# The first stage of a fused Fourier filter and MLP: first DFT in groups of 4 with two evacuations side by side, W loaded first, tables cleared by GpSimd

## Chip, cores, metric

One core of a Trainium2 chip. The time is the device time of one execution in microseconds (us), median of several executions. An interval is a 95% interval of a ratio of two kernels.

## The reference

For 8 batches of 3008 x 256: a real Fourier transform along the sequence, a complex 256 x 256 matrix with bias, a soft threshold, the inverse transform, then an MLP with a squared ReLU.

```python
def _attn_ref(x, w_r, w_i, b_r, b_i):
    X = np.fft.rfft(x, axis=1)
    Yr = Xr @ w_r - Xi @ w_i + b_r
    Yi = Xr @ w_i + Xi @ w_r + b_i
    lam = 0.01
    Yr = np.sign(Yr) * np.maximum(np.abs(Yr) - lam, 0.0)     # Yi alike
    y = np.fft.irfft(Y, n=x.shape[1], axis=1)

def _moe_ref(x, w_in, w_out, s, b):
    r = np.maximum(x @ w_in, 0.0)
    return (s * (r * r) + b) @ w_out
```

The kernel does the transform of length 3008 as 94 x 32, with tables: `A_t` for the first DFT of each column, `F_c` for the forward DFT over 32, `T_c` for its inverse, `C_t` for the last one.

## The kernel before

Only the first batch matters here. Its stages: x comes in four chunks of 8 columns (n2); each chunk gets 2 x 8 first-DFT matmuls into a PSUM tile of two banks, and four copies ("evacuations") of it into `ut`; when all of `ut` is there, the *mix* multiplies it by W; then the forward DFT needs the mix's result `g` and the table F spread out as `F_t` (by ACT) and `F_2` (by DVE).

```python
    def emit_load_x(b):
        for c in range(N2 // XCH):                     # four chunks of 8 n2
            t = xpool.tile([P, XCH * D], F16, name="x16", tag="x16")
            nc.gpsimd.dma_start(out=t[0:N1, :], in_=xv[:, c * XCH * D : (c + 1) * XCH * D])
    ...
    A_t = ...; emit_load_x(0)                          # W is not loaded here
    ...
    def first_batch():
        keep_awake(36)                                 # matmuls on ones, for the PE clock
        for c in range(N2 // XCH):
            for dc in range(DC):
                ps = two_banks()
                for j in range(XCH):
                    last_pe = nc.tensor.matmul(ps[:, j // 4, ...], x16[(0, c)][...], A_t[0:N1, :], ...)
                for h in range(2):
                    on_dve, on_act = evac(ut[:, dc, :, n2 : n2 + 4], ps[:, h, 0:384]..., 384)
            with tc.issue_after(last_pe.ins):
                keep_awake(14 if c < 3 else 10)
            if c == 0:                                 # gate: W only after the first evacuations
                with tc.issue_after(last_dve.ins):
                    for st in w_st:
                        nc.vector.memset(st[0:1, :, 0:D:P], 0.0)
                emit_load_w()
            if c == 1:                                 # gate of F_c (c == 2: T_c, the same way)
                with tc.issue_after(last_dve.ins):
                    nc.vector.memset(F_c[0:1, 0, 0, 0:1], 0.0)
                emit_load_forward()
            ...
            if c == 2:
                place_w(0)                             # ACT copies W to f16, half by half
        place_w(1); place_f(0); place_f_2(0)
```

A gate is a one-element memset of the tile to be loaded, ordered behind an evacuation: the load has to wait for it. `evac` picks ACT or DVE by a running sum of their loads.

Of the kernel before, what the change touches and what calls it, by code (L numbers as in the profile page):

```python
# [14 lines left out]
P = 128  # L15
N1 = 94
N2 = 32
# [79 lines left out]
def kernel(  # L97
# [13 lines left out]
    nc = tc.nc  # L111
    B, S, D = x.shape
# [42 lines left out]
    def evac(dst, src, cols, scale=None):  # L155
        ta, td = 0.17 + cols / 1200.0, 0.15 + cols / 960.0
        if load["act"] + ta <= load["dve"] + td:
            load["act"] += ta
            if scale is None:
                return None, nc.scalar.copy(out=dst, in_=src)  # L160
            return None, nc.scalar.mul(out=dst, in_=src, mul=scale)
        load["dve"] += td
        if scale is None:
            return nc.vector.tensor_copy(out=dst, in_=src), None
        return nc.vector.tensor_scalar_mul(out=dst, in0=src, scalar1=scale), None

    def two_banks():
        return hpool.tile([P, 2, 512], F32, name="psh", tag="psh")

    def one_bank():  # L170
        return fpool.tile([P, 512], F32, name="psf", tag="psf")

    def other_bank():
        return apool.tile([P, 512], F32, name="psa", tag="psa")


    XCH = 8
    x16 = {}

    def emit_load_x(b):  # L180
        xv = x[b].rearrange("(n1 n2) d -> n1 (n2 d)", n2=N2)
        for c in range(N2 // XCH):
            t = xpool.tile([P, XCH * D], F16, name="x16", tag="x16")
            nc.gpsimd.dma_start(  # L184
                out=t[0:N1, :], in_=xv[:, c * XCH * D : (c + 1) * XCH * D]
            )
            x16[(b, c)] = t

    ones = cpool.tile([P, P], F16, name="ones")
    nc.vector.memset(ones, 1.0)  # L190

    def keep_awake(n):

        ps = other_bank()
        for _ in range(n):
            nc.tensor.matmul(ps[:, 0:P], ones, ones, start=True, stop=True)


    A_t = cpool.tile([P, 96], F16, name="A_t")
    nc.sync.dma_start(out=A_t[0:N1, :], in_=A_d)  # L200
    emit_load_x(0)
    W_t = cpool.tile([P, DC, 2, D], F16, name="W_t")
    w_st = []
    for w in (w_r, w_i):
        st = rpool.tile([P, DC, D], F32, name="w_st", tag="rt")
        w_st.append(st)

    def emit_load_w():

        for e in (slice(0, P), slice(P, D)):  # L210
            for w, st in zip((w_r, w_i), w_st):
                nc.sync.dma_start(
                    out=st[:, :, e], in_=w.rearrange("(c p) e -> p c e", p=P)[:, :, e]
                )


    b_g = cpool.tile([P, 2, D], F32, name="b_g")
    nc.vector.memset(b_g, 0.0)
# [21 lines left out]
    def emit_load_forward():  # L240
        nc.sync.dma_start(out=F_c.rearrange("p q r k -> p q (r k)"), in_=F_d)
        nc.sync.dma_start(out=sel_t, in_=S_d)

    def emit_load_inverse():
        t_load = nc.sync.dma_start(out=T_c, in_=T_d)
        with tc.issue_after(t_load.ins):
            nc.sync.dma_start(out=eye_t, in_=E_d)
            nc.sync.dma_start(out=C_t, in_=C_d)
            for i, bv in enumerate((b_r, b_i)):
                nc.sync.dma_start(out=b_st[:, i], in_=bv.unsqueeze(0).to_broadcast([P, D]))  # L250
            nc.sync.dma_start(out=s_bc, in_=moe_s.unsqueeze(0).to_broadcast([P, 1]))
            nc.sync.dma_start(out=bb_bc, in_=moe_b.unsqueeze(0).to_broadcast([P, 1]))
# [18 lines left out]
    nc.vector.memset(T_t, 0.0)  # L271
    F_2 = [uspool.tile([P, H, P], F16, name="F_2", tag="us") for _ in range(2)]
    for f in F_2:
        nc.vector.memset(f, 0.0)

    def make_bounds():
        for t, c in ((low, -LAM), (high, LAM)):
# [11 lines left out]
    def blocks(t):  # L289
        return t.rearrange("p q (r a k) -> p q r a k", r=2, a=2)  # L290

    def place_w(ec):
        e = slice(ec * P, ec * P + P)
        for i in range(2):
            nc.scalar.copy(out=W_t[:, :, i, e], in_=w_st[i][:, :, e])

    def place_f(h):
        q = slice(h * H, h * H + H)
        for a in range(2):
            r = slice(64 * a, 64 * a + 64)  # L300
            nc.scalar.copy(out=blocks(F_t)[r, q, :, a], in_=F_c[r, q])

    def place_f_2(h):

        q = slice(h * H, h * H + H)
        for a in range(2):
            r = slice(64 * a, 64 * a + 64)
            nc.vector.tensor_scalar_mul(
                out=blocks(F_2[h])[r, :, 0, a], in0=F_c[r, q, 1], scalar1=-1.0
            )  # L310
            nc.vector.tensor_copy(out=blocks(F_2[h])[r, :, 1, a], in_=F_c[r, q, 0])
# [27 lines left out]
    def first_batch():  # L339
        ut = ypool.tile([P, DC, 96, N2], F16, name="ut", tag="yt")  # L340
        last_dve = last_act = None
        keep_awake(36)
        for c in range(N2 // XCH):
            for dc in range(DC):
                ps = two_banks()
                for j in range(XCH):
                    lo = j * D + dc * P
                    last_pe = nc.tensor.matmul(
                        ps[:, j // 4, (j % 4) * 96 : (j % 4) * 96 + 96],
                        x16[(0, c)][0:N1, lo : lo + P], A_t[0:N1, :],  # L350
                        start=True, stop=True,
                    )
                for h in range(2):
                    n2 = c * XCH + 4 * h
                    on_dve, on_act = evac(
                        ut[:, dc, :, n2 : n2 + 4],
                        ps[:, h, 0:384].rearrange("p (n k) -> p k n", k=96), 384,
                    )
                    last_dve = on_dve or last_dve
                    last_act = on_act or last_act  # L360
            with tc.issue_after(last_pe.ins):
                keep_awake(14 if c < 3 else 10)
            if c == 0:
                with tc.issue_after(last_dve.ins):
                    for st in w_st:
                        nc.vector.memset(st[0:1, :, 0:D:P], 0.0)
                emit_load_w()
            if c == 1:
                with tc.issue_after(last_dve.ins):
                    nc.vector.memset(F_c[0:1, 0, 0, 0:1], 0.0)  # L370
                emit_load_forward()
            if c == 2:
                with tc.issue_after(last_dve.ins):
                    nc.vector.memset(T_c[0:1, 0, 0:1], 0.0)
                emit_load_inverse()
            if c == 2:
                with tc.issue_after(last_act.ins):
                    place_w(0)
        with tc.issue_after(last_dve.ins), tc.issue_after(last_act.ins):
            place_w(1)  # L380
            place_f(0)
            place_f_2(0)

        gate = nc.gpsimd.tensor_copy(out=w_in_t[0][0:1, 0:1], in_=T_c[0:1, 0, 0:1])
        with tc.issue_after(gate.ins):
            emit_load_x(1)
            emit_load_weights()
# [113 lines left out]
        for i in range(2 * U + 2):  # L501
# [6 lines left out]
            k = i - U - 2  # L508
# [334 lines left out]
    def schedule(start, span, units):  # L843
        for i, u in enumerate(units):
            plan.setdefault(start + (i * span) // len(units), []).append(u)

    more = first_batch()
    load.update(act=0.0, dve=0.0)
    mark = {}
# [3 lines left out]
    schedule(0, 10, more)  # L853
    plan.setdefault(15, []).append(make_bias)
    plan.setdefault(17, []).append(lambda: emit_load_x(2))
    schedule(22, 44, s23_units(1))
    schedule(mark[1] - 14, 12, s4_units(1))
    for b in range(2, B):
        s0, s1, s2 = mark[b - 2], mark[b - 1], mark[b]
        p = s1 - s0  # L860
        schedule(s0 + 40, p - 48, s1_units(b))
        p = s2 - s1
# [47 lines left out]
```

## Time and profile before

| | before |
|---|---|
| time, median of 3 | 853.37 us (853.29 to 853.9) |
| span of the profiled execution | 852.0 us |
| PE busy | 836.7 us (98%) |
| last evacuation of `ut` ends | 16.03 us |
| first forward-DFT matmul | 18.34 us |

From 52 us on PE is full, so what the change can give is the moment at which the first batch gets through its stages. I use two marks for that: the end of the last `ut` evacuation (the first mix matmul that needs it starts 0.05 us later) and the first forward-DFT matmul. Times are from the start of the span.

### The profile page before, as it was taken

How to read it: one execution, taken by the hardware profiler on the slowest of the kernel's cores; microseconds unless marked ns; L12 is line 12 of the kernel's file. 1: busy time of each engine (PE TensorE's matmuls, PEld its weight loads, DVE VectorE, ACT ScalarE, POOL GpSimd, SP SyncE). 2: the span in 40 equal slices, each digit the busy share in tenths (PEclk: the TensorE clock that was granted, in tenths of full speed). 3: DMA queues.
4: the chain of work that ended last, by engine and by line, in shares of the span. 5: the costliest groups of instructions: out<-in, count | busy, mean ns of one | idle time of the engine just before them, and what ended most of it. 6: DMA issues, size and time to landing. Idle time of an engine off the chain costs nothing.

```text
span 852.0 us, 17108 instructions
## 1 busy us (share of the span) xinstructions
PE 836.7 (98%) x6668; PEld 602.7 (71%) x6668; DVE 698.1 (82%) x1027; ACT 643.8 (76%) x860; POOL 32.5 (4%) x54
## 2 busy tenths in 40 slices
PE   8899999999999999999999999999999999999997
PEld 7757777777777766777667776777667777766765
DVE  6888987888878987888878888888977888776674
ACT  5887887787778887787777887787877778666663
POOL 3210000000000000000000000000000000000000
PEclk9999999999999999999999999999999999999999
DMA  7963457424671357424663247613354223411111
GB/s 168 157 155 97 115 138 174 122 77 97 169 195 54 93 151 190 110 78 104 164 159 89 74 106 180 191 39 92 100 155 119 62 78 96 112 32 38 38 44 50
DMA packets 105410, 95.07 MB, mean 112 GB/s; under 512 B 9454, under 2 KB 97778, under 8 KB 103986
## 3 DMA queue, kind: packets, MB, share of 16 engines
q1 hardware_dynamic: 99330, 79.57, 32.3%
q0 software_dynamic: 6000, 14.42, 10.7%
q8 instruction: 52, 0.85, 0.4%
q14 instruction: 28, 0.23, 0.1%
HBM read 52.54 MB, written 46.66 MB: 116 GB/s over the span
## 4 chain that ended last, share of the span: by engine, by line
PE 90%; DVE 4%; ACT 3%; DMA 1%; issue 1%; DVEq 0%; ACTq 0%; POOLq 0%
PE psa L820 37%; PE psh L751 37%; PE psf L617 4%; PE psf L552 3%; PE psf L588 2%; PE psf L603 2%; PE psf L700 2%; PE psf L647 2%; DVE gt L765 1%; ACT rt L758 1%; PE psh L401 1%; DMA w_st<-in_w_r_dram 1%; DMA x<-in_x_dram 1%; ACT yt L160 0%; ACT vs L160 0%
## 5 line engine op out<-in xcount | busy, mean ns | idle before, releaser
L758 ACT ACTIVATE rt<-psh 128x1024 f32<-128x1024 f32 (+2 forms) x384 | 387.1, 1009 | 115.6 <-PE psh L751 114.2
L765 DVE TENSOR_TENSOR gt<-rt 128x1024 f16<-128x1024 f32 (+2 forms) x323 | 386.6, 1200 | 99.4 <-ACT rt L758 98.7
L820 PE MATMUL psa<-w_out_t,gt 128*128 128x256 f16 (+1 forms) x3024 | 453.9, 272 | 0.1
L820 PEld LDWEIGHTS <-gt 128*128 128x128 f16 (+1 forms) x3024 | 301.0, 101 | 186.8 <-issue 1.6
L751 PE MATMUL psh<-yt,w_in 128*128 128x512 f16 (+1 forms) x1344 | 396.9, 378 | 0.0
L751 PEld LDWEIGHTS <-w_in 128*128 128x128 f16 x1536 | 142.8, 98 | 26.6 <-issue 1.7
L830 DVE SCALAR_TENSOR_TENSOR ost<-psa,s_bc,bias_bc 128x512 f32<-128x512 f32 (+1 forms) x96 | 70.9, 738 | 9.6 <-PE psa L820 8.2
L762 ACT ACTIVATE gt<-rt 128x1024 f16<-128x1024 f32 (+2 forms) x61 | 64.1, 1051 | 1.0
L622 DVE TENSOR_TENSOR ring<-psf,s 128x512 f16<-128x512 f32 x84 | 57.5, 685 | 3.5 <-PE psf L617 3.4
L160 ACT CAST v<-psf 128x512 f16<-128x512 f32 x80 | 46.5, 582 | 18.1 <-PE psf L647 18.1
L160 ACT CAST xf<-psf 128x512 f16<-128x512 f32 x82 | 48.0, 585 | 11.1 <-PE psf L588 11.1
L160 ACT CAST u<-psf 96x512 f16<-96x512 f32 x78 | 45.1, 580 | 12.3 <-PE psf L552 12.1
L751 PE MATMUL psh<-tail,w_in 128*128 128x512 f16 (+1 forms) x192 | 52.1, 353 | 0.0
L617 PE MATMUL psf<-W_g,xf 128*128 128x256 f16 x336 | 50.4, 273 | 0.0
L160 ACT CAST yt<-psf 128x480 f16<-128x480 f32 (+2 forms) x76 | 38.5, 518 | 14.4 <-PE psf L700 14.3
L552 PE MATMUL psf<-x,A_t 94*96 94x512 f16 x104 | 39.6, 381 | 1.6 <-ACT yt L160 0.5
L628 DVE TENSOR_TENSOR ring<-ring,high 128x512 f16<-128x512 f16 x84 | 35.5, 423 | 2.2
L629 DVE TENSOR_TENSOR ring<-ring 128x512 f16<-128x512 f16 x84 | 35.5, 422 | 1.9
L627 DVE TENSOR_TENSOR ring<-ring,low 128x512 f16<-128x512 f16 x84 | 35.4, 421 | 1.5
L617 PEld LDWEIGHTS <-xf 128*128 128x128 f16 x336 | 32.9, 98 | 3.7
L184 POOL DMA_DIRECT2D x<-in_x_dram x32 | 16.9, 530 | 461.2 <-PE psf L552 445.1
L700 PE MATMUL psf<-C_t,vs 96*128 96x96 f16 x448 | 32.9, 205 | 0.0
(84 smaller groups left out, 490.7 us busy)
## 6 DMA issues: line engine op xcount, KB each, us to landing
out_dram<-ost SPq DMA_DIRECT2D x152, 128.0 KB
x<-in_x_dram POOLq DMA_DIRECT2D x32, 376.0 KB, 6.0
ud<-u SPq DMA_DIRECT2D x28, 384.0 KB
us<-ud SPq DMA_DIRECT2D x28, 384.0 KB
vd<-v SPq DMA_DIRECT2D x42, 256.0 KB
vs<-vd SPq DMA_DIRECT2D x14, 768.0 KB
ring<-ring SPq DMA_DIRECT2D x280, 32.0 KB
out_dram<-ost SPq DMA_DIRECT2D x16, 120.0 KB
```

The lines of the kernel that those rows point to most:

```text
L160: return None, nc.scalar.copy(out=dst, in_=src)
L552: nc.tensor.matmul(ps[0:96, :], A_t[0:N1, :], x16[(b, c)][0:N1, j * D : (j + 2) * D], start=True, stop=True,)
L617: nc.tensor.matmul(ps[:, r, :], xt[:, 2 - r, dc], W_g[:, dc, r], start=(dc == 0), stop=(dc == DC - 1),)
L622: nc.vector.tensor_tensor(out=t, in0=ps, in1=hold[i // 2][:, i % 2].unsqueeze(1).to_broadcast([P, 2, D]), op=ALU.add,)
L628: nc.vector.tensor_tensor(out=m, in0=m, in1=high, op=ALU.min)
L700: nc.tensor.matmul(ps[:, j * 96 : (j + 1) * 96], vs[(b, h)][:, k, ec * P : (ec + 1) * P], C_t, start=True, stop=True,)
L751: nc.tensor.matmul(o, w_in_t[dc][:, mc * P : (mc + 1) * P], r, start=(dc == 0), stop=(dc == DC - 1),)
L758: nc.scalar.activation(out=rt[:, :, 0:w], in_=ps[:, :, 0:w], func=AF.Relu)
L762: nc.scalar.activation(out=gt[:, :, 0:w], in_=rt[:, :, 0:w], func=AF.Square)
L765: nc.vector.tensor_tensor(out=gt[:, :, 0:w], in0=rt[:, :, 0:w], in1=rt[:, :, 0:w], op=ALU.mult)
L820: nc.tensor.matmul(ps[0:size, h, :], gts[(ti, mc // 2)][:, mc % 2, sub * size : (sub + 1) * size], w_out_t[:, mc, :], start=(mc == 0), sto ...
L830: nc.vector.scalar_tensor_tensor(out=ost[0:size, 0:k], in0=ps[0:size, 0:k], scalar=s_bc[0:size], in1=bias_bc[0:size, 0:k], op0=ALU.mult, o ...
```

## The change

Its intent: let ACT and DVE evacuate at the same time (a tile each), have W there before ACT needs it, start PE after half a chunk, and take clears off DVE.

```diff
@@ x in halves (batch 0 only)
+            parts = 2 if b == 0 else 1
+            for i in range(parts):
+                nc.gpsimd.dma_start(out=t[0:N1, i * w : (i + 1) * w], in_=xv[...])
@@ W at the head of the loads
         st = rpool.tile([P, DC, D], F32, name="w_st", tag="rt")
+        nc.sync.dma_start(out=st, in_=w.rearrange("(c p) e -> p c e", p=P))
-    def emit_load_w(): ...
@@ clears
     for f in F_2:
-        nc.vector.memset(f, 0.0)
+        nc.gpsimd.memset(f, 0.0)
@@ first_batch
-        keep_awake(36)
-        for c in range(N2 // XCH):
+        last_pe = keep_awake(40)
+        for g in range(N2 // 4):
+            c, h = divmod(g, 2)
             for dc in range(DC):
-                ps = two_banks()
+                ps = one_bank() if dc else two_banks()[:, 0]
...                                            (4 matmuls and one evacuation for each dc)
-                keep_awake(14 if c < 3 else 10)
+                last_pe = keep_awake(5)
+            if h == 0:
+                continue
             if c == 0:
-                ... gate of W, emit_load_w()
-            if c == 1:
                 ... gate of F_c, emit_load_forward()   # one chunk earlier
...
-            if c == 2:  place_w(0)                     # and place_w(1) at the end
+            if c == 1:  place_w()                      # whole
```

With W's gate gone, the gate of F_c moves from the second chunk to the first.

More of the change, by code (lines that the diff above doesn't have):

```diff
@@ L183, in emit_load_x @@
             t = xpool.tile([P, XCH * D], F16, name="x16", tag="x16")
-            nc.gpsimd.dma_start(
-                out=t[0:N1, :], in_=xv[:, c * XCH * D : (c + 1) * XCH * D]
-            )
+            parts = 2 if b == 0 else 1
+            w = XCH * D // parts
+            for i in range(parts):
+                nc.gpsimd.dma_start(
+                    out=t[0:N1, i * w : (i + 1) * w],
+                    in_=xv[:, c * XCH * D + i * w : c * XCH * D + (i + 1) * w],
+                )
             x16[(b, c)] = t
@@ L195, in keep_awake @@
         for _ in range(n):
-            nc.tensor.matmul(ps[:, 0:P], ones, ones, start=True, stop=True)
+            mm = nc.tensor.matmul(ps[:, 0:P], ones, ones, start=True, stop=True)
+        return mm
     A_t = cpool.tile([P, 96], F16, name="A_t")
@@ L205 @@
         st = rpool.tile([P, DC, D], F32, name="w_st", tag="rt")
+        nc.sync.dma_start(out=st, in_=w.rearrange("(c p) e -> p c e", p=P))
         w_st.append(st)
-    def emit_load_w():
-        for e in (slice(0, P), slice(P, D)):
-            for w, st in zip((w_r, w_i), w_st):
-                nc.sync.dma_start(
-                    out=st[:, :, e], in_=w.rearrange("(c p) e -> p c e", p=P)[:, :, e]
-                )
     b_g = cpool.tile([P, 2, D], F32, name="b_g")
@@ L290, in blocks, with place_w @@
         return t.rearrange("p q (r a k) -> p q r a k", r=2, a=2)
-    def place_w(ec):
-        e = slice(ec * P, ec * P + P)
+    def place_w():
         for i in range(2):
-            nc.scalar.copy(out=W_t[:, :, i, e], in_=w_st[i][:, :, e])
+            nc.scalar.copy(out=W_t[:, :, i], in_=w_st[i])
     def place_f(h):
@@ L341, in first_batch @@
         last_dve = last_act = None
-        keep_awake(36)
-        for c in range(N2 // XCH):
+        last_pe = keep_awake(40)
+        for g in range(N2 // 4):
+            c, h = divmod(g, 2)
             for dc in range(DC):
-                ps = two_banks()
-                for j in range(XCH):
-                    lo = j * D + dc * P
-                    last_pe = nc.tensor.matmul(
-                        ps[:, j // 4, (j % 4) * 96 : (j % 4) * 96 + 96],
-                        x16[(0, c)][0:N1, lo : lo + P], A_t[0:N1, :],
-                        start=True, stop=True,
-                    )
-                for h in range(2):
-                    n2 = c * XCH + 4 * h
-                    on_dve, on_act = evac(
-                        ut[:, dc, :, n2 : n2 + 4],
-                        ps[:, h, 0:384].rearrange("p (n k) -> p k n", k=96), 384,
-                    )
-                    last_dve = on_dve or last_dve
-                    last_act = on_act or last_act
+                ps = one_bank() if dc else two_banks()[:, 0]
+                with tc.issue_after(last_pe.ins):
+                    for j in range(4):
+                        lo = (4 * h + j) * D + dc * P
+                        mm = nc.tensor.matmul(
+                            ps[:, j * 96 : j * 96 + 96],
+                            x16[(0, c)][0:N1, lo : lo + P], A_t[0:N1, :],
+                            start=True, stop=True,
+                        )
+                last_pe = mm
+                on_dve, on_act = evac(
+                    ut[:, dc, :, 4 * g : 4 * g + 4],
+                    ps[:, 0:384].rearrange("p (n k) -> p k n", k=96), 384,
+                )
+                last_dve = on_dve or last_dve
+                last_act = on_act or last_act
             with tc.issue_after(last_pe.ins):
-                keep_awake(14 if c < 3 else 10)
+                last_pe = keep_awake(5)
+            if h == 0:
+                continue
             if c == 0:
-                with tc.issue_after(last_dve.ins):
-                    for st in w_st:
-                        nc.vector.memset(st[0:1, :, 0:D:P], 0.0)
-                emit_load_w()
-            if c == 1:
                 with tc.issue_after(last_dve.ins):
@@ L375, in first_batch @@
                 emit_load_inverse()
-            if c == 2:
+            if c == 1:
                 with tc.issue_after(last_act.ins):
-                    place_w(0)
+                    place_w()
         with tc.issue_after(last_dve.ins), tc.issue_after(last_act.ins):
-            place_w(1)
             place_f(0)
```

## The prediction

> **What bounds the kernel now.** I read the page first, then busy times in stretches, then the chain of waits over the first 20 us, then the order of DVE and ACT work there, then the DMA view and its packets. The stretches say where time can be won at all:
>
> ```profile
> 0.00:16.00 16.00, 12.30 (x153) 11.46 (x153) 9.21 (x21) 6.36 (x14) 3.38 (x10) 1.00 0.82 180
> 16.00:52.00 36.00, 31.14 (x381) 25.29 (x382) 31.96 (x54) 30.33 (x47) 11.21 (x16) 1.00 0.76 136
> 52.00:200.00 148.00, 147.89 (x1147) 106.34 (x1144) 127.65 (x197) 118.17 (x164) 3.08 (x6) 1.00 0.48 126
> 200.00:837.00 637.00, 635.76 (x4914) 451.94 (x4913) 523.87 (x753) 486.89 (x636) 14.81 (x22) 1.00 0.40 107
> ```
>
> The columns are stretch, length, then busy us of PE, weight loads, DVE, ACT and GpSimd, the clock, the DMA share and GB/s. From 52 us to 837 us PE is busy 783.65 of 785 us: a full pipeline that keeps its length and only moves with its start. From 16 to 52 us the first batch runs through its later stages with DVE and ACT nearly full (32 and 30 of 36 us). The change edits only what comes before that, the first DFT of batch 0. So the question is one number: when does the mix (L401, the first matmul that needs the whole of `ut`) start? Now it is 16.08 us. The chain up to there:
>
> ```profile
> 1.21 4.85 DMA x<-in_x_dram
> ...
> 6.11 1.48 PE psh L348 x16
> ...
> 8.12 0.56 DVE ut L164
> 8.67 0.05 DVE w_st L366 x2
> 8.73 4.99 DMA w_st<-in_w_r_dram
> ...
> 13.79 0.35 ACT W_t L295
> ...
> 14.60 0.39 ACT ut L160
> 14.98 0.02 issue
> 15.00 1.03 DVE ut L164 x2
> 16.04 0.05 issue
> 16.08 1.82 PE psh L401 x15
> ```
>
> Start, length, what. W is loaded only after a DVE memset at 8.67 us that itself waits for the first evacuations. It lands at 13.72, and ACT, which has the copy of W in its queue ahead of its last two evacuations, stands still for it (1.33 us). Then comes a serial tail: ACT copy, ACT evacuation, and two DVE evacuations that wait for ACT's. The list of waits up to 30 us shows that last link four times over:
>
> ```profile
> DVE ut L164 <- ACT ut L160: 5.1, 4, 2.0
> ACT W_t L295 <- DMA w_st<-in_w_r_dram: 1.3, 1, 1.3
> ```
>
> Columns: total us, times, longest. PE is not what runs late: the last eight-by-two block of first-DFT matmuls ran at 12.57 to 13.60, 2.5 us before the mix.
>
> **What the Trainium skill says.** "PSUM — Partial Sum Buffer", section "Specifications (TRN2)": ScalarE and VectorE may read PSUM at the same time at full rate if they are not in one bank. The two evacuations of a tile lie in two banks here, and DVE still waited for ACT in all four chunks; so what orders them is the shared tile, not the memory, and tiles of their own can remove it. "DMA: Bandwidth & Descriptors", section "Issuing engines are not separate DMA queues": all queues run on the same 16 engines; section "Queues, rings and completion order": an engine takes turns between queues packet by packet. The trace agrees with the first half (DMA share 1.05 while x comes in, 5 to 10 us); how x and W would share, no run shows yet. "TensorE: Matmul & The Clock Gate", section "What's actually happening": PE runs at half rate until about 3.4 us of sustained work. The trace agrees: 14 keep-awake matmuls take 1.69 us from 7.37 but 0.95 us from 10.12. "VectorE: DVE Perf Modes", section "Zero memsets can be issued as uint32": half the elements for a 2-byte type. DVE's two F clears are 128x768 uint32 in 1.51 us; on GpSimd they become 128x1536 f16.
>
> **The change, part by part.**
>
> *Evacuations side by side.* Before, a chunk of 8 n2 has two tiles, each with an ACT evacuation (0.48 to 0.53 us) and then a DVE one (0.51 to 0.60). After, a group of 4 n2 has one tile for ACT and one for DVE; the built order shows ACT always on the first, DVE on the second, and neither waiting for the other. A group costs about 0.55 us of evacuation instead of about 1.05 in series. The tail after the last matmul falls from 13.60 -> 16.03 to about one DVE evacuation.
>
> *W at the head.* The memset gate and the 4.99 us landing leave the path; ACT copies W after its fourth evacuation (2 copies of 128x512; 128x256 takes 0.41 us, so about 1.2 us together), between evacuations that ACT has time for. Removed from the path: the 1.33 us wait and, at the end, the 0.8 us of copies ahead of the last evacuations. But nothing is free on the DMA engines. x of batch 0 is 4 x 376 KB = 1.54 MB, and from 3 to 10.5 us its queue moved 1.46 MB at 99.6% of all engines, that is 0.195 MB/us: 7.9 us of pure transfer, the last packets at about 10.8 us in the packet records. In these records a 1024-byte plain packet takes 49 ns and a 3072-byte one 121 ns. W becomes 2 x 256 packets of 1024 bytes: 512 x 49 / 16 = 1.6 us of all engines. It is issued at about 1.1 us, so its packets should start near 2.2 us, and x is dense from about 2.9; I count 0.5 us of it as free and 1.1 us as taken from x.
>
> *F_c earlier.* The gate of the forward table moves from the second chunk (issue 11.44, after x) to the first, about 8 us, inside the x stream: 128 x 121 / 16 = 1.0 us more taken from x. T_c stays at the third chunk, whose packets should start about when x ends.
>
> *x in halves.* Eight loads at 0.53 us of GpSimd issue each = 4.3 us, less than the transfer, so issue is not the bound; the bytes are the same. It lets PE start after half a chunk (about 5.2 instead of 6.1) and, more to the point, leaves only 8 matmuls after the last landing instead of 16.
>
> *Clears by GpSimd.* 1.51 us leave DVE at 5.0 to 6.5, where DVE waited until 7.48 anyway: worth nothing on the path. On GpSimd, from the rows there (128x512 in 0.61 to 1.50 us) I estimate 2 to 4.5 us each, after the bias loads, so the first is done near 11 us; the half F table is needed at about 14.
>
> *Sum.* x ends at 10.8 + 1.1 + 1.0 = 12.9 us; the semaphore at about 13.1 (the first chunk shows some 0.25 us). Then 8 matmuls at 65 ns (16 take 1.03 us) and a start gap, 0.65 us; then one DVE evacuation, 0.55 us: mix at 14.3 us. Against 16.08 that is 1.8 us. Everything behind moves along: the built order of all five engines is identical, line for line, from the mix to the end. Time: 853.4 - 1.8 = 851.6, and I say 851.5.
>
> **Rivals.**
> 1. *The landing of x takes the place of the landing of W.* I hold this to be the new bound in any case; the question is how much it gives back. If W and F_c take their full 2.6 us from x and the half-size packets lose a little more, x ends at 13.5 to 14, the mix starts near 15.3 and the time is 852.6. For it: the DMA share is already 1.0. Against: W is issued before x.
> 2. *x is hardly delayed*, since W fits into the slow ramp of the x queue at 2.5 to 3.5 us and F_c packets queue behind x: x ends near 11.5, mix at 12.9, time 850.2. For it: the engines were half empty (share 0.54) in the first 5 us. Against: packet by packet turns favour the small queue's progress, at x's cost.
> 3. *W lands late instead*, because each of its packets waits for a bigger x packet: then ACT stands at the copy again, now ahead of four evacuations. If W lands by 10.5, ACT needs 1.2 + 4 x 0.48 = 3.1 us: 13.6, no harm; by 12, mix at 15.2, time 852.5.
> 4. *PE stays cold.* Groups of 8 matmuls and 5 keep-awakes take about 1.26 us at half rate (91 and 107 ns), about the spacing of the landings, so PE should look busy and warm up near 10 us as before. If not, the first mixes cost about 1.8 us more and the gain is gone: 853.4.
> 5. *The shift is lost later* to something fixed in time. T_c lands at 17.24, first use 18.20; in the new order it is issued about 2.3 us before the mix instead of 3.0, which eats most of that 1.0 us. x of batch 1 is issued after T_c and lands within 6.7 us, well before its use at 43.9; w_in lands at about 32.5, used at 50.7. So only T_c could bite, by some tenths.
>
> **Range and chances.** The chief uncertainty is the end of the x stream, 11.5 to 14 us, about 1.2 us either way; a few tenths come from the clock, T_c and the spread between runs (853.29 to 853.9). So 850.1 to 852.9. Two per cent is 17 us, more than the whole first stage: within 2% has 0.98, and the rest is for what I have not seen.
>
> **What would show it.** In the profile after: W's copies wait for no DMA or a short one; no wait of a `ut` evacuation on DVE for ACT; the waits for x in the first stage appear between groups and the last one ends near 13.1; the mix starts near 14.3; from there the distance to the end is the same 836 us within some tenths. It would be wrong if x ends before 12 or after 14, if ACT waits for W again, if the keep-awake matmuls still take 107 ns after 11 us, or if the mix moves and the end does not.

## The result, and the profile after

Ratios here and below are the mean time of one kernel's runs over that of the other's of the same rounds, so not quite the ratio of the medians quoted. Executions over 1.5% slower than the fastest of the same kernel are left out of the means.

| | before, same rounds | after |
|---|---|---|
| median of 6 | 854.37 us (853.29 to 855.13) | 854.23 us (853.3 to 856.0) |
| ratio | | 1.0001, 0.9987 to 1.0014 |
| profiled span | 852.0 us | 851.5 us |
| last `ut` evacuation ends | 16.03 us | 14.99 us |
| first forward-DFT matmul | 18.34 us | 17.38 us |

The time is the same, and above the range (850.1 to 852.9). The two profiles differ: the forward DFT is 0.96 us earlier, the end 0.48. Set side by side instruction by instruction, the changed kernel leads by 1.05 us from 25 to 108 us, by 0.82 from 113 us, by 0.81 at 837 and by 0.48 at the end; the last microseconds run at half clock in every profile, from 849.77 us before and from 848.66 after.

The stretches of the changed kernel (same columns as in the prediction):

```profile
0.00:16.00 16.00, 11.93 (x155) 10.30 (x156) 8.71 (x20) 6.85 (x12) 8.11 (x16) 1.00 0.86 191
16.00:52.00 36.00, 31.12 (x381) 24.92 (x380) 32.04 (x52) 30.41 (x49) 11.25 (x17) 1.00 0.76 139
52.00:200.00 148.00, 147.57 (x1142) 106.43 (x1141) 127.68 (x197) 118.21 (x163) 3.08 (x6) 1.00 0.47 124
```

In the first line GpSimd has the clears (8.11 us instead of 3.38) and DVE is 0.5 us lighter. The later stages keep their work, as foretold, with one exception: from 52 to 200 us PE is busy 147.57 us instead of 147.89. It stands still once, for 0.28 us (idle time and its releaser in brackets):

```profile
112.16 0.38 PE L640 MATMUL psf<-ring,T_t 128*128 128x256 f16 x2 [0.28 <-DVE ring L615]
```

There the lead falls from 1.05 to 0.82 us. The same loss of 0.22 to 0.26 us stands in every profile below (but the slow one of after_full, which is not read) that has W at the head, the groups of 4 and the GpSimd clears together, and in none of the other kernels; what delays that `ring` was not looked into.

The waits up to 30 us, to be set against those of before:

```profile
DVE ut L164 <- PE psf L346: 5.6, 8, 1.1
PEld L346 <- DMA x<-in_x_dram: 4.1, 7, 1.1
PE psh L346 <- DMA x<-in_x_dram: 2.6, 5, 0.9
ACT F_t L297 <- DMA F_c<-dft_fwd: 0.4, 1, 0.4
```

The wait of DVE's `ut` copies for ACT is gone, and so is ACT's wait for W. In their place PE and its weight loads (PEld) wait for x, up to seven times, and ACT for F_c. The chain of waits up to 20 us (start, length, what):

```profile
1.87 5.03 DMA x<-in_x_dram
...
7.50 0.56 DVE ut L164
8.06 0.04 DVE F_c L364
8.09 0.02 issue
8.11 7.00 DMA F_c<-dft_fwd
...
15.19 0.83 ACT F_t L297
16.03 0.83 ACT F_t L297
16.86 0.03 issue
16.89 1.01 ACT g L401
```

F_c, which the chain of before does not have, is in flight for 7.00 us. Its packets (in the packet records) begin only near 11 us, among the last fifth of x's; 121 of the 128 start before the last packet of x, at 13.27 us (10.93 before). The last group of first-DFT matmuls starts at 13.88, when its x has landed.

### The profile page after: what moved, and what is told of

Same layout as the page of the kernel before. It is cut to its first block, busy times and chain, and to the rows that moved or that the text cites. A ratio compares the mean times of both kernels' runs of the same rounds, so it can differ in the third digit from the quotient of the medians.

```text
span 851.5 us, 17087 instructions
## 1 busy us (share of the span) xinstructions
PE 835.2 (98%) x6660; PEld 600.6 (71%) x6660; DVE 696.7 (82%) x1023; ACT 643.2 (76%) x858; POOL 37.2 (4%) x60
## 4 chain that ended last, share of the span: by engine, by line
PE 90%; DVE 4%; ACT 3%; DMA 2%; issue 1%; POOL 0%; SPq 0%; DVEq 0%; ACTq 0%; POOLq 0%
PE psa L813 37%; PE psh L744 37%; PE psf L610 4%; PE psf L545 3%; PE psf L581 2%; PE psf L596 2%; PE psf L640 2%; PE psf L693 2%; DVE gt L758 1%; DMA F_c<-dft_fwd 1%; ACT rt L751 1%; DMA x<-in_x_dram 1%; ACT yt L160 1%; ACT vs L160 0%; PE psh L394 0%
## 5 line engine op out<-in xcount | busy, mean ns | idle before, releaser
L160 ACT CAST u<-psf 96x512 f16<-96x512 f32 x78 | 45.1, 580 | 12.4 <-PE psf L545 12.2
L187 POOL DMA_DIRECT2D x<-in_x_dram x36 | 18.9, 530 | 461.5 <-PE psf L545 445.4
```

Source lines behind the costliest of these rows:

```text
L160: return None, nc.scalar.copy(out=dst, in_=src)
```

## The experiments

Kernels of one call ran on one chip with the kernel before. All 18 gave correct results, and by its fast runs no timed one differs from the kernel before by 2%. The marks below are each from one profiled execution, and two profiles of one kernel differ in them by some tenths.

### Each part alone

**after_again**: the changed kernel once more.

> The changed kernel once more, to see how steady its profile and its time are. If the first profile was typical, the mix starts at 14.8 us again (16.08 before), everything from 17 to 113 us is 1.05 us earlier than in the kernel before and the end about 0.5 to 0.8 earlier; five rounds should then give a ratio of about 0.999, within the interval of the first measurement (0.9987 to 1.0014). If instead the first profile was a lucky one, the mix comes at 15.5 us or later and the ratio is 1.000 or more.

Measured: 854.13 us, ratio 1.0 (0.9985 to 1.0014). Last group of PE at 13.74, last evacuation ends 14.85, forward DFT 17.71: the evacuation is as early as in the first profile, but the forward DFT is not. The lead over the first profile of before is 0.73 us from 17 us, and zero at the end.

**w_only**: W at the head, everything else as before.

> W at the head of the loads alone; tiles of 8, evacuations in series, x in whole chunks, table gates and clears as before. W then costs x 1.4 to 1.6 us of DMA: x ends near 12.5 us (10.9 before). With 16 matmuls and two evacuation pairs in series after the last landing the mix comes near 15.0 to 15.3 us. If W's place were the main gain and x paid little, the mix would come at 14.0 or before.

```diff
+        nc.sync.dma_start(out=st, in_=w.rearrange(...))    # at the head; gate of W removed
-            place_w(0) / place_w(1)
+            place_w()  after the second chunk
```

Measured: 854.11 us, ratio 0.9995 (0.9976 to 1.0013). The last x packet starts at 12.17 instead of 10.93: W in front costs x 1.2 us. The last evacuation ends at 15.55, the forward DFT starts at 17.86. The wait for W is gone. What holds the end in its place is, in this execution, not x alone: PE waits for x last at 8.92 us and then works without a gap to the last group, at half clock from 8.55 to 11.96, so that 14 keep-awake matmuls end only when the last group starts at 13.48, a microsecond after x's last packet. That the landing of x takes the place of the landing of W is shown by the changed kernel's profile, not by this one.

**groups_only**: groups of 4 and halves of x; W, gates and clears as before.

> The groups of 4 with evacuations side by side and x in halves alone; loading of W, gates of the tables and the DVE clears as before. W is then asked for about 8 us and lands near 13.5 us, after x (x then ends near 11.3 as in the kernel before). If W's landing is what the old path hung on, ACT still stands at the copy of W, its last two evacuations follow at about 14.8 us, and only the serial tail shrinks: mix near 15.2 us, 0.9 us earlier than before, the same as the whole change gets (1.05 to 1.28). If moving W is what brings the gain, the mix stays at 15.8 to 16.1.

```diff
 (against the changed kernel)
-        nc.sync.dma_start(out=st, in_=w.rearrange(...))    # at the head
+            if c == 0:  # gate and load of W in four parts, as before; F_c at c == 1
+            if c == 2:  place_w(0)                         # place_w(1) at the end
-        nc.gpsimd.memset(f, 0.0)
+        nc.vector.memset(f, 0.0)
```

Measured: 854.85 us, ratio 1.0007 (0.9991 to 1.0023). PE's last group starts at 12.94, but ACT waits for W as before (to 13.61), and the last evacuation ends at 15.07. The forward DFT starts at 18.85 only: from 14.95 to 18.36 the granted clock was 0.5, over the whole first mix. So each of these two parts alone runs into a wait that the other removes: here W, in w_only the evacuations in series (14.01 to 15.55). And x in halves is not free here: its last packet starts at 12.40 us, 1.47 later than before, though W is not at the head. W was asked for 1.3 us sooner than before (7.42), and 528 of its 1024 packets start ahead of x's last one, against 113 before.

### The place of F_c

**tables_last**: F_c behind the third chunk, T_c behind the fourth.

> The changed kernel, but the forward table is asked for after the third chunk of x instead of the first, and the inverse one after the fourth. Theory A (the DMA engines are full, so the table's 1.0 us of packets comes straight out of the end of x): the last wait for x ends near 12.9 us instead of 13.88, the mix starts near 13.9. Theory B (the end of x is late for its own reasons: half-size packets, a 16 KB instruction fetch in one engine): it stays near 13.9. Theory C (the landing of the forward table, 15.11 us, has become the bound of the next stage): whatever x does, the table lands later, at 15.5 us or more, the first forward-DFT matmul stays at or after 17.4 us (17.38 in the changed kernel) and the time does not fall.

```diff
-            if c == 0:   # gate and load of F_c
+            if c == 2:
-            if c == 2:   # gate and load of T_c
+            if c == 3:
```

Measured: 853.10 us (852.64 to 853.57), ratio 0.9985 (0.9969 to 1.0000); after_again in the same rounds 854.13. Last group at 13.00, last evacuation ends 14.11, forward DFT 17.27. ACT waits 1.7 us for F_c. Theory A holds (x ends near where it said). Of C the late landing holds (the first copy of F_c starts at 15.54 us), but the forward DFT came before 17.4, and the median is lower.

**tables_last_again**: the same kernel. It was run at another time.

> If the earlier result was the version and not luck: last wait for x ends 13.0, mix 13.9, forward DFT 17.3, and 0.3 to 0.9 us under the kernel before of the same chip. Rival (luck of one profile: the 16 KB instruction packet fell behind x at 12.65 us): it falls into x's tail here, the last wait ends near 14, forward DFT near 17.7 and the median is that of before within 0.3.

Measured: 852.97 us (852.7 to 853.38), ratio 0.9978 (0.9964 to 0.9991). The profile is not as good (last group 13.29, last evacuation 14.41, forward DFT 17.98) and yet the times repeat: the profiled run took 853.38, the slowest of the five. So the forward DFT of one profile does not foretell the median.

**fc_at_second**: the changed kernel with F_c behind the second chunk, as before the change. One character of the gate.

> The changed kernel with F_c after the second chunk, as before. F_c's packets start near 12.5, behind most of x: last wait for x ends 13.0 to 13.3 instead of 13.7 to 13.9, mix 13.9 to 14.2, F_c lands about 15.3, forward DFT 17.2 to 17.5. If F_c's early place cost nothing: the last wait stays at 13.7 to 13.9. Time within 0.5 us of the changed kernel either way.

```diff
-            if c == 0:   # gate and load of F_c
+            if c == 1:
```

Measured: 853.29 us (852.98 to 854.61), ratio 0.9984 (0.9971 to 0.9997), span 851.2. Last group at 12.82, last evacuation ends 13.94, forward DFT 17.27. Its chain from 8 to 20 us:

```profile
10.21 4.78 DMA F_c<-dft_fwd
14.98 0.02 issue
15.01 0.02 ACTq L297
15.02 0.04 issue
15.07 0.83 ACT F_t L297
```

Issued 2.1 us later, F_c lands at 14.98 instead of 15.11. Its early issue bought nothing, and x's last packet started 0.95 us later for it. What the lead at the evacuation then runs into shows in the order of work (start, length, engine, line, operation, and in brackets the idle time and what ended it):

```profile
13.38 0.56 DVE L164 CAST ut<-psf 128x384 f16<-128x384 f32 x1 [0.34 <-PE psf L346]
...
15.07 1.67 ACT L297 COPY F_t<-F_c 64x768 f16<-64x768 f16 x2 [1.38 <-DMA F_c<-dft_fwd]
15.10 0.25 DVE L304 TENSOR_SCALAR F<-F_c 64x384 f16<-64x384 f16 x1 [1.16 <-DMA F_c<-dft_fwd]
...
15.99 1.23 DVE L404 TENSOR_TENSOR g<-psh,b_g 128x1024 f16<-128x1024 f32 x1
...
17.27 0.22 PE L425 MATMUL psf<-g,F_t 128*128 128x128 f16 x1 [1.57 <-DVE g L404]
```

DVE is free at 13.94, stands 1.16 us for F_c, spreads it, and only then makes `g`, for which PE waits. So F_c's landing, not the mix, sets the forward DFT here.

**fc_head**: F_c at the head of the loads, without a gate. **fc_head_placed**: the same, with its spreading behind the third chunk.

> The changed kernel with the forward table asked for at the head, right behind W and the bias rows, without a gate. Theory C (the table's landing, 15.1 to 15.5 us in the two profiles of the changed kernel, holds the next stage): the table lands before 11 us, no engine waits for it, and the first forward-DFT matmul follows the mix by 2.3 us as in the kernel before (18.34 - 16.08), against 2.6 and 3.05 in the two profiles of the changed kernel. Theory A (bytes ahead of x's end cost x their time wherever they stand): the last wait for x still ends at 13.4 to 13.9, mix at 14.3 to 14.8, first forward matmul at 16.7 to 17.1. If C is wrong, the first forward matmul stays at 17.4 to 17.7.

> The same, and the first half of the table is placed by ACT and DVE after the third chunk, in time in which they wait for x, instead of after the last evacuation. If DVE's 0.9 us of placing is on the path between the mix and the first forward matmul, that distance falls from 2.3 to about 2.2 us and the ACT copies of the first part (1.67 us) leave the stretch after the mix: first forward matmul at 16.6 to 17.0, everything behind about 1.4 us earlier than in the kernel before (1.05 and 0.73 in the changed kernel). If the copies push the last evacuations back instead, the mix comes 0.5 us or more later than in fc_head and the gain is gone.

```diff
+    nc.sync.dma_start(out=F_c..., in_=F_d)   # behind W and the bias; gate of F_c removed
-            place_f(0); place_f_2(0)         # at the end          (fc_head_placed alone)
+            if c == 2:  place_f(0); place_f_2(0)
```

Measured: 854.2 us, ratio 1.0 (0.9986 to 1.0013), and 854.82, 1.0009 (0.9995 to 1.0023). No engine waits for F_c any more, but the last x packet starts at 13.77 in fc_head, its last group at 14.93, and both kernels had a stretch of half clock (10.2 to 17.03 and 10.07 to 13.48 us). In fc_head_placed ACT did its F copies ahead of the last evacuations, which moved to 15.24 and 15.62. Forward DFT at 19.02 and 18.52: worse than the changed kernel, and both expectations were missed. With the clock in the way these two don't decide about F_c; fc_head_warm below does better.

**whole_x**: the changed kernel with x in four whole loads.

> The changed kernel with x of batch 0 in four whole loads again; groups of 4 and all else as changed. Theory B (half-size packets slow the stream): at 324 ns for 4096 bytes against 172 to 175 ns for 2048, x's stream should end 0.3 to 0.5 us sooner, near 13.4 us; against that 16 matmuls and two pairs of evacuations stand behind the last landing instead of 8 and one, 0.6 to 1.0 us more: mix at 14.8 to 15.2, so halves are worth nothing or a little. If halves cost x nothing, the mix comes 0.8 us or more later, at 15.6.

```diff
-            parts = 2 if b == 0 else 1
+            parts = 1
```

Measured: 854.39 us, ratio 1.0 (0.9987 to 1.0014). The last x packet starts at 12.23, a microsecond sooner than in halves, but both of the last groups then come after it (13.01 and 13.64): evacuation 14.75, forward DFT 17.56. The mix is 0.24 us earlier than in the changed kernel, where 0.8 later would have shown that halves cost nothing. F_c, issued at 7.85 us, has 49 of its 128 packets ahead of x's last one (121 with halves). A lead of 0.88 us (0.63 after 113 us) became a lag of 0.76 at 136 us, where PE waited 1.4 us for a load of `vs` in this execution.

### The clock

**before_again**: the kernel before, unchanged.

> The kernel before, once more with a profile. Nine timed runs of it on one chip fell in two groups: 853.1 to 853.6 us at a mean granted clock of 0.999, and 855.2 to 855.7 at 0.994 to 0.997. If the spread between runs is a stretch of 3.4 us at half clock that falls in the first 50 us or not, a profile of a run near 853.4 shows the clock whole from about 10 us on, and the mix again at 16.0 to 16.2; a profile of a run near 855.4 shows a stretch at 0.5 within the first 50 us.

Measured: 854.83 us. Two stretches of it (columns as above; the third number from the right is the granted clock), and the same two in before_full, told below:

```profile
11.86:15.27 3.41, 1.28 (x27) 1.11 (x23) 0.68 (x2) 1.90 (x6) 0.00 (x0) 1.00 0.94 326
15.27:18.68 3.41, 3.31 (x16) 2.17 (x17) 2.49 (x7) 1.94 (x3) 1.72 (x4) 0.50 0.45 78
```

```profile
11.86:15.27 3.41, 2.63 (x51) 2.46 (x48) 0.46 (x1) 1.68 (x5) 0.00 (x0) 1.00 1.01 333
15.27:18.68 3.41, 2.63 (x25) 2.11 (x26) 3.21 (x9) 3.10 (x5) 1.51 (x4) 1.00 0.42 81
```

In before_again PE was busy 1.28 of 3.41 us while it waited for W, and in the next 3.41 us the clock was 0.5: a mix matmul took 415 ns instead of 274, and the forward DFT came at 18.77. In before_full, with PE busy 2.63 us in that stretch, the clock stayed whole. This is one execution of each, and the stretches of 3.41 us that go by the clock's changes lie elsewhere in before_full (its clock rose at 6.42 us; from 13.25 to 16.66 PE was busy 2.29 us). How much work is enough the two don't tell (see the last section).

**before_warm, after_warm, fc_head_warm**: more keep-awake matmuls in the first 16 us, and fillers in the stages between 16 and 62 us.

> The kernel before with idle PE time of the first 50 us filled by matmuls on ones whose result is overwritten: 10 more at the start, 26 more ahead of the mix, 3 ahead of each inverse DFT, 4 or 2 in the last turns and the first stage of batch 1. Theory D (what spreads the runs over 853.1 to 855.7 us, and hides a gain of 1 us, is stretches of 3.4 us at half clock, granted after a stretch of that length in which PE had too little work; by my count of streamed columns the stretches that were followed by half clock were 0.31 to 0.48 full, those that were not mostly more): the clock stays whole from about 8 us on, the mean granted clock is 0.998 or more in every run, all runs lie within 0.6 us of each other near 853.4, and none near 855. If the spread has another cause, two of the five runs lie near 855 as before.

> The changed kernel filled in the same way: 9 keep-awake matmuls a group instead of 5, the rest as in before_warm. Theory D: no run near 855, the runs within 0.6 us of each other, and the gain of the change, freed of the half-clock stretches, shows as what the profiles have from 17 us on: 0.7 to 1.0 us less than before_warm, 852.4 to 852.8. Mix at 14.7 to 15.0, first forward matmul at 17.4 to 17.7, held by the forward table. If the fillers themselves cost time on the chain, both warm kernels lie above 853.6 without any half-clock stretch.

> The changed kernel with the forward table at the head and PE filled. In fc_head the table had landed by about 10.5 us and x's packets ended near 13.6, but two stretches at half clock (10.2 to 17.0 us) put the mix at 16.1 to 16.3. Without them: last wait for x ends at 13.6 to 13.9, mix at 14.5 to 14.8, first forward matmul 2.3 us later at 16.8 to 17.1, everything behind 1.3 to 1.5 us earlier than in the first profile of the kernel before, and a time of 852.0 to 852.4, the best of all. If the first forward matmul stays at 17.4 or later, the table was not what held it.

```diff
-                last_pe = keep_awake(5)            # before_warm: 36 -> 46 at the head, 10 -> 36 at the end
+                last_pe = keep_awake(9)
+            fill(ps, n)   # n = 2 to 4 matmuls on ones ahead of the later stages' own
```

Measured: 855.91, 855.52 and 856.14 us, ratios 1.0027, 1.0021 and 1.0023 to before. The expected times failed, and what was named for after_warm as the other case came true: the clock was whole from 7 us on, but the fillers themselves cost 1.4 to 1.9 us between 38 and 62 us. What they show is the first stage under a whole clock: evacuation and forward DFT at 15.61 and 17.92 before, 15.39 and 17.70 after, 16.10 and 18.42 with F_c at the head. In the last, F_c waits for nobody, and the distance is 2.32 us: so it is F_c's landing that makes it longer elsewhere. But x, with F_c ahead of it, starts its last packet at 14.01, and nothing is won.

**before_full, after_full, last_full, last_whole_full**: fillers in the first 16 us alone, for before, after, tables_last, and tables_last with whole x.

> The kernel before with more keep-awake matmuls in the first 16 us and nothing else. Half-clock theory: the mix at 15.2/15.7, first forward DFT at 17.9, no half-clock window before 45 us in most executions, so the group of runs at 855 thins out and the median is about 853.4. Rival (the slow group comes from DMA stalls later on): the two groups stay and the median stays within 0.3 us of the kernel before.

> The changed kernel with 9 keep-awake matmuls a group instead of 5. Theory (x's end late by W, halves and F_c; F_c's own landing next): last wait for x ends 13.7 to 14.3, mix 14.7 to 15.2, first forward DFT 17.4 to 17.7, so 0.2 to 0.5 us under before_full at that point, and a median of 853.0 to 853.3. Rival (the prediction's 1.8 us is there once the clock is full): forward DFT at 16.5 and a median near 851.6.

> As after_full, with F_c after the third chunk and T_c after the fourth. Theory: x ends 0.8 us earlier than in after_full (last wait ends about 13.0), mix 13.9, F_c lands about 15.5 and T_c about 17.7, forward DFT 17.2 to 17.3; median 852.7 to 852.9, 0.2 to 0.4 under after_full. Rival (F_c's place makes no difference to the end): same as after_full within 0.1.

> As last_full with x in four whole loads. If the half-size packets of x cost time on the DMA engines, the last x packets end near 11.4 instead of 12.4, the last two groups run by 12.9, mix near 13.8 and F_c (issued earlier) lands near 15.0; forward DFT about 17.0, median about 852.6. Rival (what counts is the wait for F_c, whose issue hangs on DVE after the third chunk): no difference to last_full beyond 0.1.

```diff
-        keep_awake(36) ... keep_awake(14 if c < 3 else 10)     # before_full
+        keep_awake(46) ... keep_awake(14 if c < 3 else 36)
-                last_pe = keep_awake(5)                        # the other three
+                last_pe = keep_awake(9)
```

before_full: 853.62 us, ratio 0.9999 (0.9985 to 1.0013); evacuation 15.83, forward DFT 18.15. Four of its five runs lie in the lower group of times (see below); six of nine of before in the same rounds did too, so the filling proves nothing about the groups.

after_full: 855.43 us (855.39 without the slow run), ratio 1.0014 (1.0 to 1.0028). One of its runs, the profiled one, took 970.48 us at a clock of 0.851 all through; nothing is read from it. The four others (853.55 to 855.94) don't reach the expected 853.0 to 853.3.

last_full: 854.5 us (854.2 to 854.78), ratio 1.0007 (0.9994 to 1.0019), where I expected 852.7 to 852.9. tables_last itself had 853.10 and 852.97, so four more matmuls a group go with 1.4 us more. The last group starts at 14.19 instead of 13.00, and then another table is late:

```profile
14.74 0.56 DVE ut L164
15.30 0.04 DVE T_c L368
15.34 0.02 issue
15.36 3.09 DMA T_c<-dft_inv
...
18.54 0.35 DVE T_t L314
...
20.01 1.23 DVE g L404
```

The forward DFT is still early (17.69), but DVE waits for T_c, whose gate hangs on the late last evacuation, and the second `g` comes at 20.01; behind it the execution is 0.55 us later than before_full. In the packet records one 16384-byte instruction packet takes 936 ns from 12.11 us, and the two last x packets start at 13.03 and 13.19, and take 233 and 281 ns instead of 173. In tables_last that packet came at 12.65, after x. That it held up x is what the order suggests; the records don't say which engine a packet ran on, and in tables_last_again it came at 11.99 with the last group at 13.29.

last_whole_full: 854.9 us, ratio 1.0011 (0.9999 to 1.0024); evacuation 14.75, but F_c was issued at 13.10 and its copies start at 16.14, forward DFT 18.34. Expected were 17.0 and 852.6 us: missed.

**last_whole**: tables_last with whole x, keep-awakes of 5.

> x in four whole loads, both tables behind x, keep-awakes of 5. With whole packets the last x packets end near 12.1 instead of 12.4, last two groups at 12.6 and 13.2, mix 13.9 to 14.2; F_c issued about 12.8, lands 15.5 to 16, forward DFT 17.3 to 17.8. Rival (halves cost and whole loads gain): x ends 11.5, mix 13.4. Time 852.8 to 853.6.

Measured: 854.8 us, ratio 1.0 (0.9986 to 1.0015), an expectation missed. The last x packet starts at 12.08, yet PE, whose clock rose only at 13.74 in this execution, ends late: evacuation 15.40, F_c issued at 13.92, forward DFT 18.68.

## Why the prediction was wrong

The profiled executions without half clock over the mix fit one account: the forward DFT starts 2.3 us after the last evacuation (2.31 in before, w_only, before_warm and after_warm, 2.32 in fc_head_warm), unless F_c is late, and then later. The medians are of different chips, so they are not to be compared down the column.

| | last x packet starts | last evacuation ends | forward DFT | difference | median us |
|---|---|---|---|---|---|
| before | 10.93 | 16.03 | 18.34 | 2.31 | 854.37 |
| before_full | 10.71 | 15.83 | 18.15 | 2.32 | 853.62 |
| w_only | 12.17 | 15.55 | 17.86 | 2.31 | 854.11 |
| after | 13.27 | 14.99 | 17.38 | 2.39 | 854.23 |
| after_again | 13.14 | 14.85 | 17.71 | 2.86 | 854.13 |
| tables_last | 12.42 | 14.11 | 17.27 | 3.16 | 853.10 |
| tables_last_again | 12.71 | 14.41 | 17.98 | 3.57 | 852.97 |
| fc_at_second | 12.32 | 13.94 | 17.27 | 3.33 | 853.29 |

**Right.** The bound of the kernel and where a gain could come from; evacuations of 0.48 and 0.56 us side by side; no wait for W; the GpSimd clears off the path (done at 10.37 us, at 1.40 us each and not 2 to 4.5). The first rival, x in the place of W, with an end of x at 13.5 to 14 and 852.6 us, was nearer than the main line.

**The step that failed: "x ends at 10.8 + 1.1 + 1.0 = 12.9 us; the semaphore at about 13.1".** The last x packet ended at 13.27 + 0.17 = 13.44, PE began at 13.88, and the last evacuation ended at 14.99 instead of 14.3 (mix 15.04). The 0.69 us by terms: the last packet of before started at 10.93, not 10.8 (0.13), and I took its start for its end (0.17); W and F_c together with the halves cost x 13.27 - 10.93 = 2.34 us instead of 2.1 (0.24); from the last packet's end to the first matmul it is 0.44 us instead of 0.2 (0.24); matmuls and evacuation took 1.11 us instead of 1.2 (-0.09). W's share is 1.24 us (w_only) and F_c's 0.95 (after against fc_at_second), near the 1.1 and 1.0. But F_c costs that only with x in halves: with whole loads x ends at 12.23 with F_c in its stream (whole_x) and at 12.17 or 12.08 without (w_only, last_whole). "The bytes are the same" missed that. The packet records show how: with halves 121 of F_c's 128 packets start before the last of x, with whole loads 49; W's do the same in groups_only (528 of 1024, 113 before). Why halves let other loads in, no run settles.

**"Everything behind moves along."** It does not, and the prediction's own sign of being wrong came true: the mix moved and the end did not. Between mix and forward DFT lies F_c. The fifth rival named only T_c. I had F_c's earlier issue as a cost to x (1.0 us, rightly), and took for granted that it would land earlier for it; it did not (15.11, against 14.98 when issued 2.1 us later). In the first profile after, F_c cost 0.08 us (2.39 against 2.31), in the second 0.55, and in the kernels with x freed of it 0.85 and 1.0. Later on 0.23 us go at 112 us and 0.33 in the last microseconds.

**"Against 16.08 that is 1.8 us."** The profile that I subtracted from was a rather slow one of its kind: its PE ran at half clock until 10.09 us. Other profiles of before have their last evacuation at 15.61 to 15.83 (before_again, and with PE filled before_warm and before_full), and the two filled ones their forward DFT at 17.92 and 18.15. So, from profile to profile, the change brings the forward DFT forward by 0.2 to 1.0 us, not 1.8, and part of it is gone at the end.

**The time itself.** From the first profile of before to that of after, the predicted 1.8 us became 1.04 at the mix, 1.05 at 25 us, 0.82 at 113 us and 0.48 at the end. The rest of the miss lies between runs. Of the 53 runs of before in these rounds, 28 lie between 853.14 and 853.94 us and 25 between 854.43 and 856.22; the three of the first table were all of the lower group, so 853.4 was not the median to subtract from. After has 5 of 11 runs at 854.36 or more. The profiled run of after was its fastest of six (853.3), so its span of 851.5 shows the change at its best; over all runs the gain is not there, and the interval of 0.9987 to 1.0014 allows about 1.1 us either way.

**What takes it away, and how sure that is.** Shown, by one profile of each: undoing the one line that moves F_c brings the evacuation 1.05 us forward. Seen for two orders of loads: with F_c later, 13 of 14 runs (tables_last twice, fc_at_second) are at 853.57 or less, with medians of 852.97 to 853.29, and 854.13 for the changed kernel in the rounds it shares with tables_last. It is not true of every late F_c: last_full, last_whole and last_whole_full have it late too, with medians of 854.5 to 854.9. The two orders are 0.15 to 0.22% under before in the rounds they share. Part of that is the upper group of before; against its lower group alone, whose runs lie around 853.5, it is 0.2 to 0.5 us. Half-clock stretches of 3.41 us that cost 1 to 2 us are shown in single profiles of before, groups_only and others. Not shown by experiment: that they make the upper group of times. For it speaks the record of the granted clock, kept for 47 of the runs of before: 23 of the 25 in the lower group have 0.999, and none of the 22 in the upper (0.994 to 0.998). Against it, or at least not for it: before_full did not separate the groups, all runs of last_full are at 854.2 to 854.78 with 0.998 to 1.0, and tables_last_again was fast with a half-clock stretch from 8.98 to 12.4 us, where PE waited for x anyway. Why tables_last loses its 1.4 us with four more keep-awakes lies, in the one profile of last_full, in a later end of x and then in T_c; what made x late there is open.

## What to carry to other kernels

When the DMA engines are full, a load moved forward can be paid by the load that is needed first (F_c by x here, with x in halves): ask for each table when it is used, and whether it lands any sooner for being issued sooner. Follow the chain past the wait that you remove, to the next table or semaphore, before you carry a gain to the end. And take the baseline from several profiles when a gain of a microsecond is at stake: here one kernel's runs lie 2 us apart.

## What the Trainium skill lacked or had wrong

- "TensorE: Matmul & The Clock Gate", section "What's actually happening", has the free-running window of 3413 ns and says the clock falls after an idle one. It lacks how much work counts as idle, and PE's busy time alone does not give it. With the windows laid from where each execution's clock changed, the clock fell to 0.50 after windows with PE busy 1.28 (before_again), 1.64 (w_only), 1.71 (groups_only), 1.90 (tables_last_again) and 1.95 us (fc_head), and not after 1.78 (before), 1.84 (last_full) and 1.90 us (whole_x).
- "DMA: Bandwidth & Descriptors", section "Queues, rings and completion order": an engine drains a whole packet of many descriptors before it turns to another queue. My "packet by packet" misread this as one record at a time. The trace after fits the page: W and x move in turns of many records, 169 and 9 from 2.9 to 3.5 us, 25 and 79 from 3.5 to 4.5, 127 and 7 from 4.5 to 5.0. What the page doesn't give is what it means for a landing: F_c took 7.00 us issued into the stream of x and 4.78 us issued 2.1 us later.
- "Runtime: NRT & Kernel Launch", section "Instruction fetch mechanics", has instruction blocks of this size, but lacks how long one takes beside other loads: here a packet of 16384 bytes on the queue marked "instruction" took 878 to 1052 ns, at 11 to 13.5 us in all these kernels, among the last packets of x or just behind them.
- No page has a time for the clear of 128x1536 f16 by GpSimd: 1.40 us (two in 2.71 us).
